# Gated linear attention and an ELU layer on one core: P3's bank and P5's sum, turns ahead of P7, squares and table load inside the layer, the weights' sums ahead of unit 2's layer

## The chip, the cores and the metric

The kernel runs on one core of one Trainium2 chip. The core has a matrix engine (TensorE, PE in the profile), a vector engine (VectorE, DVE), an engine for activation functions and copies (ScalarE, ACT), a general engine (GpSimd, POOL) and an engine that issues most of the transfers (SyncE, SP). Each works through its own list of instructions in order, and they wait for each other by semaphores. The metric is the device time of one execution, in microseconds (us). Lower is better.

## The reference

The first half is a gated linear attention with a complex decay. For 4 sequences of 8 heads, 768 steps and 48 channels per head:

```python
mag = sqrt(a_re*a_re + a_im*a_im);  scale = minimum(mag, 0.999) / (mag + 1e-6)
a_re_n, a_im_n = a_re*scale, a_im*scale
for t in range(S):                       # S_re, S_im: 48 x 48 per head
    new_re = ar*S_re - ai*S_im;  new_im = ar*S_im + ai*S_re
    S_re, S_im = new_re + outer(k[t], v[t]), new_im
    y[t] = q[t] @ S_re
```

The heads are then laid side by side, which gives x of 3072 tokens by 384, and the second half is

```python
h = x @ w_in                             # 384 x 2048
g = where(h > 0, h, exp(minimum(h, 0)) - 1)
out = g @ w_out                          # 2048 x 384
```

All is in float32.

## The kernel before, in words

**Units.** The work is cut into 12 units of two sequences and 128 steps each, numbered 0 to 11. A unit goes through three stages: the attention, which gives x; the layer, which multiplies x by w_in and applies the ELU, and gives g; and the products, which multiply g by w_out. Units 0 and 1 do layer and products directly (`inner`, `elu`, `project`). Unit 2 has the direct layer but the saving products, and units 3 to 11 have saving forms of both: fewer block products with sums of blocks before and behind.

**The attention of a unit.** `squares` (L709, L710, ACT) squares a_re and a_im, `joined` (L716) adds them, `logarithms` and `powers` take logarithms and exponentials (each with a load of the activation table), `ratios`, `lengths` and `slopes` work on them (DVE), `angles` (L815, ACT) takes the arctangent, `carried` (L826, DVE, one row) adds what the unit before left. `turned` (called by `turns`) sums the angles along time by a matrix product (L837, PE) and takes off whole turns (L842, L845, DVE), and `carry_on` (L862, POOL) stores the last row for later. `waves` (L973, L976, L977, ACT) makes sine and cosine. `decays` gives the decay factors E and F, `ends` (L957, POOL) loads the decays at the chunks' ends, `scaled` (L982 on POOL for k, L992 on DVE for q) multiplies by them, and `gated` (L1003, DVE for q, POOL for k) multiplies by the waves. Then q and k are transposed on PE (L1023) and copied by ACT (L1024), `scored` and `valued` make scores, states and outputs, and `seam` moves rows into place by transfers. `noted` (L796, L799, DVE) keeps the extremes of a for a later test, and the tiles of a exist once, so that `load_a` of the next unit waits for the last reader of this one, which is `noted`.

**The layer of units 3 to 11.** `mixed` and `mixed_rest` (L1409, L1429, DVE; L1432, POOL) make sums of x's blocks. Twenty multiplications (`mult`, L1449, four matrix products each, in the order of `ORDER`: 8, 1, 6, 3, 9, 7, 5, ...) add into five PSUM banks called b, z, w, x and y. Three of the banks come from a ring of three ("mlp") that the products also use. Where a bank's sum is wanted before more is added to it, ACT copies it (`kept`, L1462): z after multiplications 8 and 1, ahead of 3, and w after 6. `joint` (L1465, DVE) combines, and `low` and `whole_of` (L1470, L1471, L1474) apply the ELU, which needs the table of exponentials (`table`, L1200). The weights' side needs block sums too: 19 sums of w_in (`summed_in`) and 8 of w_out (`combined`, L1278), made once on DVE. `opened` takes over buffers that were in use before, for some of these.

**The products of units 2 to 11.** Seven block products, P1, P4, P2, P5, P6, P7, P3 in this order, each in two halves (`product`, L1319). P1 and P2 add up in columns 0 of the first bank and P6 takes columns 1 of it; P5 has columns 0 of another bank and P7 columns 1; P4 has the third. P3 adds onto P5. ACT copies P1 (L1327), DVE adds P6 to it (u2), then P7 (u3, L1344), and the four quarters of the output are: P1 + P2 (L1338, ACT), u2 + P5 + P3, u3 + P5 and u3 - P4 (L1340, DVE). Each goes out by a transfer (L1341).

**Order.** The order of the work is written by hand. A list, `first`, gives the beginning up to unit 2's layer. Behind it every step has a time in slots (`put`), 16 slots for a unit, and the steps are issued in the order of these times, each onto its engine. Unit u starts from r = 16(u - 2). While unit w's layer runs (r + 36 to r + 44) and its products (r + 44 to r + 52), the attention of unit w + 2 is under way at the same slots: with its own r, the products of unit w lie at r + 12 to r + 20, and the layer of unit w + 1 at r + 20. The turns of unit w + 2 at r + 18.32 so come behind P7, and the squares of unit w + 3, at its own r + 3.4, come just before the layer of unit w + 1. Between these, parts of the weights are fetched again and tested for small values (`test_fetch`, L666 and L669, SP; `test`, L680, DVE): 48 of them.

Of the kernel before, what the change touches and what calls it, by code (L numbers as in the profile page):

```python
# [13 lines left out]
ALU = mybir.AluOpType  # L14
# [491 lines left out]
def kernel(  # L506
# [12 lines left out]
    nc = tc.nc  # L519
# [53 lines left out]
    def work(shape, tag="w"):  # L573
        return ps.tile(shape, FP32, tag=tag, bufs=3, name=tag)
# [4 lines left out]
    def where(u):  # L579
        return u % (B // NB) * NB, u // (B // NB) * C  # L580
# [78 lines left out]
    done, tested = [], []  # L659
# [33 lines left out]
    def new(tag, bufs=1, shape=None):  # L693
        return sb.tile(shape or [C, NB, H, D], FP32, tag=tag, bufs=bufs, name=tag)
# [314 lines left out]
    PAIRED = 2  # L1009
# [239 lines left out]
    HN = DM // 2  # L1249
    spare, P = [], NF // 2  # L1250

    def Y(j, n):
        return w_out.rearrange("p (m j) n -> p m j n", j=2)[:, :, j, ts(n, HN)]
# [12 lines left out]
    def T_of(k, h):  # L1266

        if k == 4:
            return spare[4 + h]
        return (spare[2] if k == 1 else spare[3] if k == 2 else Y(0, 1))[:, ts(h, P // 2)]  # L1270
# [9 lines left out]
    def X(u, h, i, j):  # L1280
        return nat[u]["g", h].rearrange("p (m j) (i t) -> p m j i t", j=2, i=2)[:, :, j, i]

    def S_of(u, k, h):

        if k == 3:
            return spare[1][:, 0 : P * C].rearrange("p (m t) -> p m t", t=C)[:, ts(h, P // 2)]
        return X(u, h, *{1: (1, 0), 2: (0, 0), 4: (0, 1)}[k])
# [11 lines left out]
    def product(u, k, h):  # L1299

        x = nat[u]
        bank, n, first = {
            1: (0, 0, True), 2: (0, 0, False), 6: (0, 1, False), 5: (1, 0, True),
            7: (1, 1, False), 3: (1, 0, False), 4: (2, 0, True),
        }[k]
        if first and h == 0:
            x["p", bank] = work([C, 2, HN], "mlp")
        to = x["p", bank][:, n]
        a = {
            1: lambda: X(u, h, 0, 0), 2: lambda: X(u, h, 0, 1), 3: lambda: S_of(u, 4, h),  # L1310
            4: lambda: X(u, h, 1, 1), 5: lambda: S_of(u, 1, h), 6: lambda: S_of(u, 2, h),
            7: lambda: S_of(u, 3, h),
        }[k]()
        if k < 4:
            b = Y(*((0, 0), (1, 0), (1, 1))[k - 1])[:, ts(h, P // 2)]
        else:
            b = T_of({4: 4, 5: 1, 6: 2, 7: 3}[k], h)
        for m in range(P // 2):
            nc.tensor.matmul(  # L1319
                to, lhsT=a[:, m], rhs=b[:, m], start=(first and h == 0 and m == 0), stop=False,  # L1320
                skip_group_check=True,
            )
        if h == 0 or k in (4, 5):
            return
        if k == 1:
            x["u"] = new("ee", 2, [C, 2, GT])
            nc.scalar.copy(out=x["u"][:, 0, 0:HN], in_=to)  # L1327
            return
        u2, u3 = (x["u"][:, n, 0:HN] for n in range(2))
        if k == 6:  # L1330
            nc.vector.tensor_tensor(out=u2, in0=to, in1=u2, op=ALU.add)
            return
        seq, at = where(u)

        def done(i, n, a, b, op=None):
            o = new("o", 2, [C, HN])
            if op is None:
                nc.scalar.copy(out=o, in_=a)  # L1338
            else:
                nc.vector.tensor_tensor(out=o, in0=a, in1=b, op=op)  # L1340
            nc.sync.dma_start(out=out[ds((seq + i) * S + at, C), ts(n, HN)], in_=o)  # L1341

        if k == 7:
            nc.vector.tensor_tensor(out=u3, in0=to, in1=u2, op=ALU.add)  # L1344
            done(1, 1, u3, x["p", 1][:, 0], ALU.add)
            done(1, 0, u3, x["p", 2][:, 0], ALU.subtract)
        elif k == 2:
            done(0, 0, to, None)
        else:
            done(0, 1, to, u2, ALU.add)  # L1350


    ROLES = (1, 0), (1, 1), (0, 0), (0, 1)
# [125 lines left out]
    def verdict():  # L1479
# [31 lines left out]
        out=ident, in_=ident, pattern=[[-1, C]], base=0, channel_multiplier=1,  # L1511
# [42 lines left out]
    def put(at, fn, *args):  # L1554
        if fn is hidden:
            plan.append((at, len(plan), inner, args))
            plan.append((at, len(plan), elu, args))
        else:
            plan.append((at, len(plan), fn, args))

    def decays_of(u, *at):
        fns = squares, joined, logarithms, powers, lengths, ratios, slopes, noted, angles, carried
        if u > 3:
            put(at[6] + 0.3, carry_back, u)
        put(at[0], begun, u)
        for x, fn in zip(at, fns):
            put(x, fn, u)

    def gates_of(u, *at):
        for x, fn in zip(at, (decays, turns, waves, scaled, ends, gated)):  # L1570
            if fn is not decays or u <= PAIRED:
                put(x, fn, u)
# [47 lines left out]
        (ratios, 3), (project, 0, 0, 8, 12), (transposed, 2, "k", 0), (transposed, 2, "q", 1),  # L1620
        (slopes, 3), (angles, 3), (project, 1, 1, 12, 16), (transposed, 2, "k", 1),
        (carried, 3), (scored, 2), (turns, 3), (project, 0, 1, 8, 12), (valued, 2), (seam, 2),
        (noted, 3), (project, 0, 0, 12, 16), (waves, 3), (scaled, 3), (ends, 3),
        (project, 0, 1, 12, 16), (opened,),
    ]
    def layer_of(u, at_h, at_p):
        if u == PAIRED:
# [33 lines left out]
        for m, (k, h) in enumerate(ks):  # L1661
            put(at_p + m * step, product, u, k, h)
# [3 lines left out]

    for u in range(2, NU):
        r = (u - 2) * SLOTS
        put(r + (1.5 if u > PAIRED else 8), load_a, u)
        put(r + 8, load_v, u)  # L1670
        put(r + 8, load_qk, u)
        if u == 2:
            decays_of(u, 16, 16, 17, 17, 18.4, 19.5, 19.6, 22.7, 19.8, 19.8)
            gates_of(u, 20.4, 21.6, 22.1, 22.4, 22.4, 22.6)
        else:
            sq = (r + 7.2, r + 9.6) if u == PAIRED + 2 else (r + 3.4, r + 5)
            decays_of(u, *sq, r + 12.8, r + 13.2, r + 13.4, r + 13.5, r + 14.9, r + 15.7, r + 15.52, r + 16.6)
            gates_of(u, r + 15, r + 18.32, r + 18.5, r + 18.6, r + 18)
            put(r + 19.7, gated, u, None, ("q",))
            put(r + 19.8, gated, u, None, ("k",))  # L1680
            if u > PAIRED + 1:
                put(r + 19.45, table, "exp_and_others", u)
                put(r + 15.5, table, "trig_and_small", u)
            if u > PAIRED + 1:
                put(r + 16.8, scaled, u, "k", None)
        if u > PAIRED:
            for n in range(NB):
                put(r + 22 + 2 * n, transposed, u, "q", n)
                put(r + 23 + 2.3 * n, transposed, u, "k", n)
            at = r + (31.3 if u + 1 < NU else 30.6)  # L1690
            put(r + 28.2, scored, u)
            put(at, valued, u)
            put(at, seam, u)
            put(r + 34.45, mixed, u)
            put(r + 35.75, mixed_rest, u)
        layer_of(u, r + 36, r + 44)
    for n in range(len(SUMS)):
        put(37 + 0.6 * n if n < 11 else 45.4 + 0.6 * (n - 11), summed_in, n)
    for m, x in enumerate(((1, 0), (2, 0), (1, 1), (4, 0), (2, 1), (4, 1), (3, 0), (3, 1))):
        put(37.2 + m * 0.6 if m < 6 else 40 + m, combined, *x)  # L1700
    for m in range(NR):
        put(40 + 2.75 * m, test_fetch, m)
        put(42.2 + 2.75 * m, test)
    put(NU * SLOTS, verdict)
    items = [(fn, tuple(args)) for fn, *args in first]
    items += [x[2:] for x in sorted(plan, key=lambda x: x[:2]) if x[2:] not in items]
# [38 lines left out]
```

## Time and profile before

| | |
|---|---|
| runs of the kernel | 701.9 us median of 3 (700.37 to 706.64) |
| profiled execution | 701.03 us, of which the span is 699.3 us |
| mean granted clock of TensorE | 0.973 |
| PE, matrix products | 651.5 us busy, 93% of the span |
| DVE | 498.9 us, 71% |
| ACT | 418.9 us, 60% |
| POOL | 156.5 us, 22% |
| transfers | 56.12 MB, mean 80 GB/s |
| chain that ended last | PE 58%, DVE 15%, ACT 14% of the span |
| first multiplication of the layers of units 3 to 11 | 228.00, 278.69, 331.77, 388.60, 443.17, 495.98, 550.33, 604.39, 654.04 us |

A page of the profile shows one execution. The span is the time from its first instruction to its last. Each engine's busy time is the union of its instructions. The rows of slices cut the span into 40 equal pieces, and a digit is the busy share in tenths, or for PEclk the share of full clock that TensorE was granted. In the waits, "A <- B: total, times, longest" says that A's engine was idle until B ended. In the timeline a row has the start, the length, the engine, the line and operation, and in brackets the idle time of the engine ahead of it and what ended it.

### The profile page before, as it was taken

What the parts mean: (1) busy time and instruction counts of PE and PEld (TensorE: products, weight loads), DVE (VectorE), ACT (ScalarE), POOL (GpSimd) and SP (SyncE); (2) the same over time, 40 slices, a digit from 0 to 9 for tenths busy, and PEclk for the clock granted to TensorE, in tenths of its full rate; (3) what the DMA queues carried; (4) which work ended last, traced back from release to release, by engine and by line L of the source; (5) the groups of instructions that cost most, each with busy time, mean ns of one, the idle gap of its engine ahead of it and who ended that gap; (6) DMA issues with size and microseconds to landing.
All of it is one profiled execution on the core that took longest, in us unless ns stands there. A gap on an engine that the chain in (4) does not pass through costs nothing.

```text
span 699.3 us, 17222 instructions
## 1 busy us (share of the span) xinstructions
PE 651.5 (93%) x7236; PEld 591.3 (85%) x7236; DVE 498.9 (71%) x790; ACT 418.9 (60%) x684; POOL 156.5 (22%) x200
## 2 busy tenths in 40 slices
PE   8898889999997999899799899899899899999995
PEld 6777776577886998898799899899899899899995
DVE  5889999863979587487477668578568658755381
ACT  6875446847753775765567577477377477472250
POOL 2000000122114324324304403503502501502000
PEclk9899999999998999999899999999999999999999
DMA  9985646322815605603433242342620641210000
GB/s 167 169 162 104 157 137 177 57 64 45 136 39 79 119 17 98 122 17 70 97 70 74 72 75 64 74 100 60 125 51 24 129 71 31 60 31 13 18 1 29
DMA packets 151443, 56.12 MB, mean 80 GB/s; under 512 B 129684, under 2 KB 143164, under 8 KB 151356
## 3 DMA queue, kind: packets, MB, share of 16 engines
q1 hardware_dynamic: 147616, 53.58, 38.1%
q0 software_dynamic: 3520, 1.20, 1.5%
q8 instruction: 59, 0.97, 0.6%
q14 instruction: 28, 0.23, 0.1%
q10 hardware_dynamic: 220, 0.14, 0.1%
HBM read 48.91 MB, written 4.80 MB: 77 GB/s over the span
## 4 chain that ended last, share of the span: by engine, by line
PE 58%; DVE 15%; ACT 14%; issue 4%; DMA 4%; SPq 4%; ACTq 0%; DVEq 0%
PE mlp L1319 13%; PE mlp L1449 11%; PE y L1449 8%; PE mlp L1210 6%; PE w L1023 5%; PE mlp L1235 3%; SPq L598 3%; PE y L1235 3%; PE w L1064 3%; PE y L1109 2%; DMA ai<-in_a_im_dram 2%; PE y L1136 2%; ACT L1200 2%; DVE g L1297 1%; ACT L735 1%
## 5 line engine op out<-in xcount | busy, mean ns | idle before, releaser
L1319 PE MATMUL mlp<-w_out,g 128*128 128x192 f32 x640 | 116.2, 333 | 2.8 <-DVE o L1340 2.8
L1319 PEld LDWEIGHTS mlp<-w_out,g 128*128 128x128 f32 x640 | 106.8, 194 | 6.5 <-DVE o L1340 5.1
L1081 POOL TENSOR_TENSOR S<-S,T 128x384 f32<-128x384 f32 x36 | 33.1, 920 | 198.0 <-DVE S L1079 198.0
L1465 DVE TENSOR_TENSOR g<-g,mlp 128x512 f32<-128x512 f32 x45 | 30.9, 686 | 59.5 <-PE mlp L1449 42.1
L1210 PE MATMUL mlp<-x,w_in 128*128 128x256 f32 x288 | 65.1, 381 | 3.2 <-DVE g L1221 2.3
L1210 PEld LDWEIGHTS mlp<-x,w_in 128*128 128x128 f32 x288 | 53.8, 190 | 11.9 <-DVE g L1221 2.7
L1297 DVE TENSOR_TENSOR g<-g 128x512 f32<-128x512 f32 x80 | 59.4, 753 | 5.7 <-PE mlp L1319 4.7
L1449 PE MATMUL mlp<-x,w_in 128*128 128x128 f32 x432 | 58.9, 281 | 0.0
L1319 PE MATMUL mlp<-w,g 128*128 128x192 f32 x320 | 54.7, 329 | 0.0
L1449 PEld LDWEIGHTS mlp<-x,w_in 128*128 128x128 f32 x432 | 54.5, 198 | 0.0
L1319 PEld LDWEIGHTS mlp<-w,g 128*128 128x128 f32 x320 | 51.8, 190 | 0.7
L1474 DVE SCALAR_TENSOR_TENSOR g<-ee,g 128x512 f32<-128x512 f32 x63 | 43.8, 696 | 11.2 <-ACT ee L1471 11.1
L1024 ACT COPY qt<-w 128x512 f32<-128x512 f32 x48 | 25.9, 589 | 40.7 <-PE w L1023 40.7
L1470 ACT ACTIVATE ee<-g 128x512 f32<-128x512 f32 x63 | 39.5, 627 | 17.3 <-DVE g L1465 16.9
L973 ACT ACTIVATE cs<-n 128x768 f32<-128x768 f32 (+1 forms) x14 | 10.5, 751 | 63.6 <-DVE n L845 63.6
L1471 ACT ACTIVATE ee<-ee 128x512 f32<-128x512 f32 x72 | 45.4, 631 | 2.3
L1190 POOL DMA_DIRECT2D x<-y x62 | 29.9, 489 | 59.5 <-ACT y L1126 37.2
L1449 PE MATMUL mlp<-halves,g 128*128 128x128 f32 x144 | 22.5, 305 | 17.9 <-ACT g L1462 17.9
L1449 PEld LDWEIGHTS mlp<-halves,g 128*128 128x128 f32 x144 | 19.8, 213 | 19.4 <-ACT g L1462 19.4
L904 ACT ACTIVATE n<-w 64x384 f32<-64x384 f32 (+1 forms) x60 | 28.1, 486 | 8.9 <-PE w L889 8.3
L1462 ACT COPY g<-mlp 128x512 f32<-128x512 f32 x36 | 20.4, 586 | 21.3 <-PE mlp L1449 21.2
L1449 PE MATMUL y<-x,w_in 128*128 128x128 f32 x216 | 31.9, 295 | 0.0
(218 smaller groups left out, 1442.3 us busy)
## 6 DMA issues: line engine op xcount, KB each, us to landing
w<-in_moe_w_out_dram SPq DMA_DIRECT2D x8, 768.0 KB, 4.4
g<-in_moe_w_in_dram SPq DMA_DIRECT2D x24, 256.0 KB, 3.1
g<-in_moe_w_out_dram SPq DMA_DIRECT2D x24, 256.0 KB, 2.9
w<-in_moe_w_in_dram SPq DMA_DIRECT2D x16, 288.0 KB, 5.7
vn<-in_v_dram SPq DMA_DIRECT2D x24, 192.0 KB, 4.3
out_dram<-o SPq DMA_DIRECT2D x48, 96.0 KB, 2.7
ar<-in_a_re_dram SPq DMA_DIRECT2D x22, 192.0 KB, 3.5
ai<-in_a_im_dram SPq DMA_DIRECT2D x22, 192.0 KB, 4.8
```

What stands on the lines that cost most here:

```text
L1023: nc.tensor.transpose(t[:, h], of, ident)
L1081: eng.tensor_tensor(out=new_s, in0=new_s, in1=wide, op=ALU.mult)
L1190: eng.dma_start(out=x["x"][ds(j * HP + D, G), i], in_=x["y"][ds(j * HP + i * G, G)])
L1210: nc.tensor.matmul(t[:, e], lhsT=w_in[:, i, ts(f + e, C)], rhs=x["x"][:, i], start=(i == 0), stop=(i == NI - 1),)
L1235: nc.tensor.matmul(x["o", n], lhsT=x["g", f // 8][:, f % 8, ts(n, C)], rhs=w_out[:, f], start=(f == 0), stop=(f == NF - 1),)
L1297: nc.vector.tensor_tensor(out=S_of(u, k, h), in0=a, in1=b, op=op)
L1319: nc.tensor.matmul(to, lhsT=a[:, m], rhs=b[:, m], start=(first and h == 0 and m == 0), stop=False, skip_group_check=True,)
L1449: nc.tensor.matmul(x["c" + c][:, ts(m, C)], lhsT=a[:, m], rhs=x["mix"][p], start=(p == BANKS[c][0] and m == 0), stop=False, skip_group_che ...
L1465: nc.vector.tensor_tensor(out=part(u, to), in0=part(u, a), in1=part(u, b), op=op)
L1470: nc.scalar.activation(out=e, in_=part(u, of), func=AF.Relu, scale=-1.0)
L1471: nc.scalar.activation(out=e, in_=e, func=AF.Exp, scale=-1.0)
L1474: nc.vector.scalar_tensor_tensor(out=part(u, to), in0=nat[u]["e", to], scalar=-1.0, in1=part(u, of), op0=ALU.add, op1=ALU.max,)
```

## The change

- `product`: P3 starts a sum of its own in columns 0 of the bank that P1 and P2 had. Behind P6, DVE makes one more sum, u4 = u2 + P5. The outputs are then P3 + u4, P7 + u4, and (P7 + u2) - P4, the last in two steps.
- `turns` and `waves` go from r + 18.32 and r + 18.5 to r + 17.2 and r + 17.4, ahead of P7; the gates of q and k go from r + 19.7 and r + 19.8 to r + 18.7 and r + 18.8, and `mixed_rest` goes one slot ahead, in front of P3's second half.
- `squares` and `joined` go from r + 3.4 and r + 5 to r + 5.08 and r + 6 for units from 6 on, and to r + 7.2 and r + 9.6 for unit 5. (Unit 4 had the latter already, and unit 3's are in `first`.) The table load behind them goes from r + 19.45 to r + 21.1 for units from 6 on.
- `load_a` of unit 5 goes from r + 1.5 to r + 4.5, and `noted` of unit 4 from r + 15.7 to r + 20.3.
- `opened`, three of the sums of w_in and six of the sums of w_out move into `first`, ahead of the end of unit 0's last product, so ahead of unit 2's layer.
- The weight tests start 14 slots later, and follow each other at 2.5 slots in place of 2.75.

```diff
-            7: (1, 1, False), 3: (1, 0, False), 4: (2, 0, True),
+            7: (1, 1, False), 3: (0, 0, True), 4: (2, 0, True),
         }[k]
-        if first and h == 0:
+        if first and h == 0 and k != 3:
             x["p", bank] = work([C, 2, HN], "mlp")
...
-        u2, u3 = (x["u"][:, n, 0:HN] for n in range(2))
+        u2, u4 = (x["u"][:, n, 0:HN] for n in range(2))
         if k == 6:
             nc.vector.tensor_tensor(out=u2, in0=to, in1=u2, op=ALU.add)
+            nc.vector.tensor_tensor(out=u4, in0=x["p", 1][:, 0], in1=u2, op=ALU.add)
             return
 
-        def done(i, n, a, b, op=None):
+        def done(i, n, a, *sums):
             o = new("o", 2, [C, HN])
-            if op is None:
+            if not sums:
                 nc.scalar.copy(out=o, in_=a)
-            else:
+            for b, op in sums:
                 nc.vector.tensor_tensor(out=o, in0=a, in1=b, op=op)
+                a = o
...
         if k == 7:
-            nc.vector.tensor_tensor(out=u3, in0=to, in1=u2, op=ALU.add)
-            done(1, 1, u3, x["p", 1][:, 0], ALU.add)
-            done(1, 0, u3, x["p", 2][:, 0], ALU.subtract)
+            done(1, 1, to, (u4, ALU.add))
+            done(1, 0, to, (u2, ALU.add), (x["p", 2][:, 0], ALU.subtract))
...
-            done(0, 1, to, u2, ALU.add)
+            done(0, 1, to, (u4, ALU.add))
...
-        (noted, 3), (project, 0, 0, 12, 16), (waves, 3), (scaled, 3), (ends, 3),
-        (project, 0, 1, 12, 16), (opened,),
+        (noted, 3), (project, 0, 0, 12, 16), (opened,), (waves, 3), (summed_in, 0),
+        (summed_in, 1), (combined, 1, 0), (combined, 2, 0), (summed_in, 2), (combined, 1, 1),
+        (combined, 4, 0), (combined, 2, 1), (scaled, 3), (combined, 4, 1), (ends, 3),
+        (project, 0, 1, 12, 16),
...
-        put(r + (1.5 if u > PAIRED else 8), load_a, u)
+        put(r + (8 if u == PAIRED else 4.5 if u == PAIRED + 3 else 1.5), load_a, u)
...
-            sq = (r + 7.2, r + 9.6) if u == PAIRED + 2 else (r + 3.4, r + 5)
-            decays_of(u, *sq, r + 12.8, r + 13.2, r + 13.4, r + 13.5, r + 14.9, r + 15.7, r + 15.52, r + 16.6)
-            gates_of(u, r + 15, r + 18.32, r + 18.5, r + 18.6, r + 18)
-            put(r + 19.7, gated, u, None, ("q",))
-            put(r + 19.8, gated, u, None, ("k",))
+            sq = (r + 7.2, r + 9.6) if u < PAIRED + 4 else (r + 5.08, r + 6)
+            noting = r + (15.7 if u != PAIRED + 2 else 20.3)
+            decays_of(u, *sq, r + 12.8, r + 13.2, r + 13.4, r + 13.5, r + 14.9, noting, r + 15.52, r + 16.6)
+            gates_of(u, r + 15, r + 17.2, r + 17.4, r + 18.6, r + 18)
+            put(r + 18.7, gated, u, None, ("q",))
+            put(r + 18.8, gated, u, None, ("k",))
             if u > PAIRED + 1:
-                put(r + 19.45, table, "exp_and_others", u)
+                put(r + (19.45 if u < PAIRED + 4 else 21.1), table, "exp_and_others", u)
...
-            put(r + 35.75, mixed_rest, u)
+            put(r + 34.75, mixed_rest, u)
...
-        put(40 + 2.75 * m, test_fetch, m)
-        put(42.2 + 2.75 * m, test)
+        put(54 + 2.5 * m, test_fetch, m)
+        put(56 + 2.5 * m, test)
```

More of the change, by code (lines that the diff above doesn't have):

```diff
@@ L1328, in product @@
             return
-        u2, u3 = (x["u"][:, n, 0:HN] for n in range(2))
+        u2, u4 = (x["u"][:, n, 0:HN] for n in range(2))
         if k == 6:
             nc.vector.tensor_tensor(out=u2, in0=to, in1=u2, op=ALU.add)
+            nc.vector.tensor_tensor(out=u4, in0=x["p", 1][:, 0], in1=u2, op=ALU.add)
             return
         seq, at = where(u)
-        def done(i, n, a, b, op=None):
+        def done(i, n, a, *sums):
             o = new("o", 2, [C, HN])
-            if op is None:
+            if not sums:
                 nc.scalar.copy(out=o, in_=a)
-            else:
+            for b, op in sums:
                 nc.vector.tensor_tensor(out=o, in0=a, in1=b, op=op)
+                a = o
             nc.sync.dma_start(out=out[ds((seq + i) * S + at, C), ts(n, HN)], in_=o)
         if k == 7:
-            nc.vector.tensor_tensor(out=u3, in0=to, in1=u2, op=ALU.add)
-            done(1, 1, u3, x["p", 1][:, 0], ALU.add)
-            done(1, 0, u3, x["p", 2][:, 0], ALU.subtract)
+            done(1, 1, to, (u4, ALU.add))
+            done(1, 0, to, (u2, ALU.add), (x["p", 2][:, 0], ALU.subtract))
         elif k == 2:
-            done(0, 0, to, None)
+            done(0, 0, to)
         else:
-            done(0, 1, to, u2, ALU.add)
+            done(0, 1, to, (u4, ALU.add))
     ROLES = (1, 0), (1, 1), (0, 0), (0, 1)
```

## The prediction

> **What bounds the kernel now.** I read the page's busy shares first, then the waits of TensorE alone, then the timeline of ACT and of PE around one of those waits, and last the granted clock there.
>
> ```profile
> PE 651.5 (93%) x7236; PEld 591.3 (85%) x7236; DVE 498.9 (71%) x790; ACT 418.9 (60%) x684; POOL 156.5 (22%) x200
> ...
> PEclk9899999999998999999899999999999999999999
> ```
>
> TensorE is the bound: 93% busy, and every other engine has room. So only two things can shorten the run: less idle PE, and fewer stretches at a lowered clock (the 8s of the clock row).
>
> ```profile
> PE mlp L1449 <- ACT g L1462: 17.9, 7, 3.8
> PE w L837 <- DVE n L826: 3.5, 1, 3.5
> PE mlp L1319 <- DVE o L1340: 2.8, 3, 1.1
> ```
>
> These are the three longest waits of PE: total us, times, longest. The first is one place in each of seven layers. The timeline shows it at the layer of 388.60 us, ACT first (start, length, what, idle before), then PE:
>
> ```profile
> 388.07 0.84 ACT L973 ACTIVATE cs<-n 128x768 f32<-128x768 f32 x1 [6.83 <-DVE n L845]
> 388.82 0.83 ACT L976 ACTIVATE cs<-n 128x768 f32<-128x768 f32 x1
> 389.69 0.94 ACT L977 ACTIVATE cs<-cs,quarter 128x768 f32<-128x768 f32 x1
> 390.53 0.83 ACT L709 ACTIVATE n<-ar 128x768 f32<-128x768 f32 x1
> 391.26 0.83 ACT L710 ACTIVATE n<-ai 128x768 f32<-128x768 f32 x1
> 392.11 1.28 ACT L1200 ACT_TABLE_LOAD   x1
> 393.40 1.07 ACT L1462 COPY g<-mlp 128x512 f32<-128x512 f32 x2
> ```
>
> ```profile
> 382.11 2.76 PE L1319 MATMUL mlp<-w_out,g 128*128 128x192 f32 x16
> 384.71 1.45 PE L837 MATMUL w<-n,sum_turns 128*128 128x384 f32 x4
> 386.00 2.76 PE L1319 MATMUL mlp<-w_out,g 128*128 128x192 f32 x16
> 388.60 1.05 PE L1449 MATMUL mlp<-x,g 128*128 128x128 f32 x8
> 389.50 1.06 PE L1449 MATMUL mlp<-halves,g 128*128 128x128 f32 x8
> 390.39 1.06 PE L1449 MATMUL mlp<-x,w_in 128*128 128x128 f32 x8
> 394.04 1.16 PE L1449 MATMUL mlp<-halves,g 128*128 128x128 f32 x8 [2.59 <-ACT g L1462]
> ```
>
> PE runs P7, the turns' product, P3, then the layer's first three multiplications, and stops: the fourth adds onto a bank that ACT must first copy (kept). ACT sat idle for 6.83 us until DVE had made the angles, then did sine, absolute value and cosine, two squares and a table load before the copy. The copy was wanted at 390.4 and began at 393.4.
>
> ```profile
> 391.40:394.00 2.60, 0.04 (x1) 0.00 (x0) 1.91 (x3) 2.57 (x4) 0.88 (x2) 1.00 0.11 38
> 394.00:399.30 5.30, 5.26 (x32) 5.26 (x33) 1.70 (x3) 0.69 (x2) 4.75 (x2) 0.68 0.15 49
> ```
>
> In this table by stretch the first figures are length and PE busy; the third from the right is the granted clock. After 2.6 us without work it is 0.68 for the next 5.3 us.
>
> **The change, part by part.**
>
> Turns ahead of P7. P6 ends at 382.11. The angles' row (DVE L826) ran 381.27 to 382.22, so L837 can start at about 382.37 (in the trace L837 at 220.08 followed L826's end at 219.94 by 0.15): a wait of 0.26 that is not there now. It ends at 383.66. The four DVE steps behind it take 2.2 us (385.84 to 388.04 in the trace); from 383.2, when the first half is there, they end near 385.4, where today they end at 388.04. P7's three results no longer stand ahead of them. ACT's three waves take 2.46 us (388.07 to 390.53) and are done by 387.9. P7 and P3 end at 388.86, the multiplications 8 and 1 at 390.65: ACT is free 2.8 us before the copy is wanted, 1.5 us in layer 4, where the table load stays ahead of it. So the wait goes in all seven layers, squares moved or not; moving them adds 2.9 us more cover. The carry DMA of turns now stands on POOL ahead of the two DMAs of ends (1.9 us of issue); what those bring is read only by the state sums of the next unit, over 30 us later.
>
> What the wait costs: the seven gaps are 2.60, 3.79, four of 2.59 and 1.12, together 17.9. To that comes the clock: it is at 0.50 for 6.8 us from 337.5 and for 3.4 us each from 395.5, 501.4 and 556.0, and at half speed half of that is lost, 3.4 + 3 x 1.7 = 8.5. Here a rule speaks against so large a sum: the Trainium skill, "TensorE: Matmul & The Clock Gate", Part 1, throttles only after an idle window of about 3.4 us. By it only the gap of 3.79 would cost clock, and the sum would be 21.3. But three of the five gaps of 2.6 us have a slow stretch behind them, so the row decides: 26.4. As a cross-check, layers 4 to 10 begin at 278.69, 331.77, 388.60, 443.17, 495.98, 550.33 and 604.39; with 53.08 - 2.75 = 50.33 as the undisturbed spacing (its layer lost only the gap), these six spacings hold 23.7 too much, and the 1.3 of layer 10 makes 25.0. I take 25.0.
>
> P3 in P2's bank, P5 added to u2. P3 need not wait for P7's results. Today L837 hides that wait (no gap at 386.00); with L837 gone from there it would be 0.84 a layer, as at 650.50 and 689.31, so this part pays for the first. But u4 reads P5 from the bank that P7 writes. The Trainium skill ("PSUM — Partial Sum Buffer", PSUM bank collisions) has banks guarded as a whole, other columns too, so P7 must wait for u4: two DVE additions behind P6, like the 0.84 above. By the skill that is 0.84, without its rule 0. In the products of units 2 to 9 L837 with its 1.29 us lies between and hides it; in those of units 10 and 11, which have no turns beside them, 0.84 is paid at P7 in place of P3: net 0. One more DVE addition per unit (0.3 us) lies beside PE. P2's copy by ACT is done some 12 us before P3.
>
> Squares and table within the layer. In layers 4 to 9 two squares (1.66) and, from layer 5, the table (1.28) stand between the two first copies and the copies of the q transposes. From the layer's start: second copy ends at 3.4, squares at 5.0, table at 6.3; the first half of the transposes is there at about 6.0. ACT falls 0.3 behind, and the copy before multiplication 12 has 0.1 of room (348.63 to 349.21, wanted at 349.33). The squares also need ai landed: in the trace it lands, where a landing is recorded, between 4.1 us before a layer's start and 3.1 after. Behind the squares on ACT stand the table, all transposes' copies and every later kept copy, and PE waits for those. On DVE the gate of q (1.75) and the pair sum (0.42) now stand ahead of P3's result, whose bank multiplication 7 takes: P3's result at about 4.2 after the layer's start, multiplication 7 wants it at 4.5. POOL's gate of k ends near 7.9, its transposes come at 8.0. Cost of these thin covers: 0 to 1.2 a layer (each being missed by a few tenths); I take 0.3, since layer 3 today, begun at 228.00 with nothing late, shows no gap above 0.2. 7 x 0.3 = 2.1. For unit 5 alone the squares stand between k's copies and the copy before multiplication 12, where ACT is already full: 1.7.
>
> Weights' sums ahead of unit 2's layer. Nine sums, three of 0.6 and six of 0.87, 7.0 us of DVE. They go where DVE idles today: 8.27 us before 166.81 (waiting for ACT L904) and 2.60 before 171.23. Cost 0. Out of the layer they free DVE: the gap of 0.80 at 195.80 (PE for DVE L1079) goes. The layer itself (166.66 to 190.99) has no gap now, so nothing is won in it. What matters comes at 216.56: PE waits 3.52 for L826, then 1.09 for P3's results, then runs slowly (0.50 from 221.5 for 6.8 us). From P6's end at 213.80 to the next layer at 228.00 are 14.20 us for 6.49 of work: 7.7 lost. The change takes two reductions (0.86 each) and a weight test (0.33) from before L826, but asks for it 2.6 us sooner. L826 ends between 215.7 and 217.1 with P6 at 213.0: the wait is 2.8 to 4.2 with 0 to 3.4 of clock behind it. I take 3.5 + 1.7 = 5.2, a gain of 2.5 (0 to 4.9).
>
> Load of a for unit 5 and weight tests later: the load has 9 us until its squares, with 6.4 from issue to landing at worst; tests leave 184 to 228 and squeeze a little later, where DVE has 29% free. 0.
>
> Sum: 25.0 + 2.5 + 0.8 - 7 x 0.26 - 2.1 - 1.7 = 22.7. The profiled execution took 701.0 (span 699.3 and 1.7 around it), 0.9 below the median: 701.0 - 22.7 = 678.3, and with that 0.9, 679 us.
>
> **The rivals.**
>
> Thin covers miss everywhere: 1.2 us in each of eight layers, 9.6 in place of 2.1, gives 687. For it: four covers of 0.1 to 0.4. Against it: they overlap, and a gap on one gives room to the next.
>
> The wait moves instead of going: L826 comes late each time, so PE waits at L837 as it now waits at the copy, about 2.6 in seven units (18 on top of 679), with 0 to 4 of clock: some 697 to 701. For it: unit 2's product, where just this happens today. Against it: in the other seven L826 ends 0.11 after P6, released by ACT L815, with DVE waiting for it.
>
> Slower: squares meet an unlanded ai inside the layer. Then ACT is blocked behind them, and copies that PE needs stop too. It breaks even with today once a load lands some 6.5 us after the layer's start, giving about 3 us of gap and 1 of clock in six layers; at 9 us it is 6 x 6.5 = 39 on top of 678, some 717. For it: one load in the trace (issued at 328.5 us, behind a weight test) lands 3.1 after its layer's start. Against it: the tests' new places put no test between most loads and what they wait for.
>
> The edit falling short (P3 still waiting, 0.84 x 7) would give 685, within the second case.
>
> **How the numbers follow.** Forecast 0.62 (671 to 684: unit 2's gain from 0 to 4.9, covers from 0 to 0.7, clock by chance), thin covers 0.20 (684 to 692), the wait moved 0.10 (692 to 703), slower 0.08. Range 671 to 692. About 1% (7 us) is what a measurement tells from no change. Faster by more 0.85, within it 0.07, slower 0.08.
>
> **What would show it.** PE's wait for the kept copy under 3 us in all; layers about 50.5 to 51 us apart; L973 at least 3 us before its layer's first multiplication; L837 after P6 with gaps of 0.2 to 0.4, and one of 3 to 4 near 213; no slow clock at layers' starts. It is wrong if PE waits at L837 by over 1 us in most units, if PE waits at multiplications 7 or 12 or at transposes by over 1 us a layer, or if ACT L710 waits for ai.

## The result, and the profile after

The changed kernel takes 680.6 us (median of four runs, 677.98 to 685.29), where the kernel before takes 702.25 (median of four, 700.37 to 706.64). The ratio is 0.969, with a 95% interval from 0.962 to 0.976: faster by about 22 us. The profiled execution took 677.98, its span 676.2. Two rows of its page, the busy shares and the granted clock:

```profile
PE 642.4 (95%) x7236; PEld 581.7 (86%) x7236; DVE 502.3 (74%) x800; ACT 419.1 (62%) x684; POOL 157.8 (23%) x200
...
PEclk9799999999998999999999999999999999999998
```

PE stays the bound and is busy for 9 us less, though it has the same 7236 instructions: what is gone is time at half speed (the mean granted clock went from 0.973 to 0.986). Between the start and the last slice only one slow slice is left. In the clock's records behind 100 us, before had six slow stretches ahead of the end; now there is one, of 6.8 us, from 214.0.

The first multiplications of layers 3 to 11 now stand at 224.43, 276.93, 327.33, 378.31, 428.58, 478.91, 530.41, 580.36 and 630.08. From the first to the last of them it is 405.7 us where it was 426.0: 20.4 of the 23.1 us of span. 3.6 were won ahead of layer 3, some of it chance (a slow stretch from 105.4 us, in code that did not change, is missing now), and 0.9 were lost behind layer 11.

The waits of PE after (total us, times, longest):

```profile
PE w L837 <- DVE n L826: 4.3, 1, 4.3
PE y L1450 <- ACT g L1463: 4.0, 4, 1.8
...
PE mlp L1319 <- DVE ee L1332: 1.8, 2, 0.9
```

The multiplications are at L1450 now and kept's copy at L1463, one line further down. The wait of 17.9 us ahead of the fourth multiplication is gone from the list. The one layer in detail, ACT and then PE (start, length, what, idle before):

```profile
376.51 0.94 ACT L977 ACTIVATE cs<-cs,quarter 128x768 f32<-128x768 f32 x1
380.29 0.59 ACT L1463 COPY g<-mlp 128x512 f32<-128x512 f32 x1 [2.85 <-PE mlp L1450]
381.18 0.59 ACT L1463 COPY g<-mlp 128x512 f32<-128x512 f32 x1 [0.31 <-PE mlp L1450]
381.67 0.85 ACT L709 ACTIVATE n<-ar 128x768 f32<-128x768 f32 x1
```

```profile
371.74 1.53 PE L837 MATMUL w<-n,sum_turns 128*128 128x384 f32 x4
373.11 5.36 PE L1319 MATMUL mlp<-w_out,g 128*128 128x192 f32 x32
378.31 1.05 PE L1450 MATMUL mlp<-x,g 128*128 128x128 f32 x8
...
380.98 1.10 PE L1450 MATMUL mlp<-halves,g 128*128 128x128 f32 x8
```

Now ACT waits for PE: it has finished the waves and is idle for 2.85 us until the sum that it copies exists. P7 and P3 run as one stretch of 5.2 us, and the fourth multiplication comes 2.67 us behind the first, with no gap.

### The profile page after: what moved, and what is told of

The parts are those of the page before. It is cut to its first block, busy times and chain, and to the rows that moved or that the text cites. A ratio compares the mean times of both kernels' runs of the same rounds, so it can differ in the third digit from the quotient of the medians.

```text
span 676.2 us, 17220 instructions
## 1 busy us (share of the span) xinstructions
PE 642.4 (95%) x7236; PEld 581.7 (86%) x7236; DVE 502.3 (74%) x800; ACT 419.1 (62%) x684; POOL 157.8 (23%) x200
## 4 chain that ended last, share of the span: by engine, by line
PE 53%; DVE 11%; ACT 9%; issue 4%; DMA 2%; SPq 0%; DVEq 0%; ACTq 0%
PE mlp L1319 18%; PE mlp L1450 9%; PE y L1450 6%; PE w L1023 4%; PE mlp L1210 3%; PE w L1064 3%; PE y L1109 3%; DVE g L1466 2%; PE w L837 2%; PE y L1136 2%; DVE g L1475 2%; PE mlp L1235 2%; ACT L735 2%; ACT n L746 1%; DVE g L1297 1%
## 5 line engine op out<-in xcount | busy, mean ns | idle before, releaser
L1319 PE MATMUL mlp<-w_out,g 128*128 128x192 f32 x640 | 113.3, 331 | 1.8 <-DVE ee L1332 1.8
L1210 PEld LDWEIGHTS mlp<-x,w_in 128*128 128x128 f32 x288 | 53.8, 190 | 11.3 <-DVE g L1221 2.8
L1297 DVE TENSOR_TENSOR g<-g 128x512 f32<-128x512 f32 x80 | 57.7, 731 | 5.0 <-PE mlp L1319 3.8
L1466 DVE TENSOR_TENSOR g<-g,mlp 128x512 f32<-128x512 f32 x45 | 30.7, 683 | 38.2 <-PE mlp L1450 23.9
L1450 PE MATMUL mlp<-x,w_in 128*128 128x128 f32 x432 | 57.2, 275 | 0.0
L1450 PEld LDWEIGHTS mlp<-x,w_in 128*128 128x128 f32 x432 | 52.6, 192 | 0.0
L1463 ACT COPY g<-mlp 128x512 f32<-128x512 f32 x36 | 21.2, 588 | 43.4 <-PE mlp L1450 43.2
L1450 PE MATMUL y<-x,w_in 128*128 128x128 f32 x216 | 29.3, 278 | 4.0 <-ACT g L1463 4.0
L1450 PEld LDWEIGHTS y<-x,w_in 128*128 128x128 f32 x216 | 26.2, 192 | 4.9 <-ACT g L1463 4.8
L1219 ACT ACTIVATE ee<-mlp 128x512 f32<-128x512 f32 x24 | 14.3, 595 | 25.6 <-PE mlp L1210 16.8
```

Of the source, the lines that this page charges most:

```text
L1210: nc.tensor.matmul(t[:, e], lhsT=w_in[:, i, ts(f + e, C)], rhs=x["x"][:, i], start=(i == 0), stop=(i == NI - 1),)
L1297: nc.vector.tensor_tensor(out=S_of(u, k, h), in0=a, in1=b, op=op)
L1319: nc.tensor.matmul(to, lhsT=a[:, m], rhs=b[:, m], start=(first and h == 0 and m == 0), stop=False, skip_group_check=True,)
L1450: nc.tensor.matmul(x["c" + c][:, ts(m, C)], lhsT=a[:, m], rhs=x["mix"][p], start=(p == BANKS[c][0] and m == 0), stop=False, skip_group_che ...
L1466: nc.vector.tensor_tensor(out=part(u, to), in0=part(u, a), in1=part(u, b), op=op)
```

## The experiments

The theory: what was lost before was ACT's lateness at the kept copy, and the clock behind it. The rivals: that the gain comes from the product's new banks, or from the weights' sums. The change has parts that can be undone, or done alone. The runs come from three rounds of measuring, in which the kernel before had medians of 702.25 (with the changed kernel), 699.72 (the first four below) and 700.92 (the last four). So a difference of 2 us between medians of different rounds tells nothing.

**The product alone.** On the kernel before, only P3's bank and u4:

```diff
-            7: (1, 1, False), 3: (1, 0, False), 4: (2, 0, True),
+            7: (1, 1, False), 3: (0, 0, True), 4: (2, 0, True),
...
+            nc.vector.tensor_tensor(out=u4, in0=x["p", 1][:, 0], in1=u2, op=ALU.add)
...
```

> Only P3's bank and P5's sum, on the kernel before; turns, squares, tables, sums and tests stay. If P7 must wait for u4 because both are in one bank, PE waits about 0.84 us between P6 and P7 in the products of units 3 to 11, since L837 stands behind P7 here: slower than before by about 0.84 x 8 = 7 us, some 708 to 710. If other columns of a bank are free, nothing changes: 701 to 703.

Measured: 708.18 us (706.1 to 712.34), ratio 1.012 (1.005 to 1.020). The waits of its PE:

```profile
PE mlp L1450 <- ACT g L1463: 19.3, 8, 2.6
PE mlp L1319 <- DVE ee L1332: 15.1, 10, 7.3
```

Alone this part costs time. P7 waits for u4 in each of the ten products: 0.84 to 0.98 where nothing else is in the way, and 7.3 in unit 2's, where u4 stands behind L826 in DVE's full queue. So in this program P7 does wait for a reader of other columns of its bank; whether the hardware would need that wait, no run shows. The kept wait stays: 2.59 in seven layers, layer 3 now among them, and 1.13 in one.

**All but the product.** The changed kernel with the product of before:

```diff
-            7: (1, 1, False), 3: (0, 0, True), 4: (2, 0, True),
+            7: (1, 1, False), 3: (1, 0, False), 4: (2, 0, True),
...
```

> The changed kernel with the product as before: P3 adds onto P5, u3 is back. With L837 ahead of P7, P3 follows P7 directly and has to wait for P7's results, about 0.84 us in each of the products of units 2 to 9 where the changed kernel has no wait: about 0.84 x 8 = 7 us over the changed kernel, some 687. If this part pays nothing, 679 to 682.

Measured: 684.9 us (682.18 to 688.46), ratio 0.978 (0.970 to 0.985).

```profile
PE mlp L1319 <- DVE o L1340: 8.4, 10, 0.8
```

P3 now waits 0.84 ten times, in place of 0.91 twice at P7. That is the expected 7 us in the waits. The medians lie 4 us apart, between the two cases, and their ranges overlap. What the expectation left out are the waits of the layer's y bank for a copy by ACT (L1449 <- L1462; L1450 <- L1463 in the changed kernel): they are 1.2 us in all here, and 4.0 in the changed kernel.

**All but the turns.**

```diff
-            gates_of(u, r + 15, r + 17.2, r + 17.4, r + 18.6, r + 18)
+            gates_of(u, r + 15, r + 18.32, r + 18.5, r + 18.6, r + 18)
```

> The changed kernel with turns and waves back behind P7 (18.32 and 18.5). If moving squares and table is enough for the kept copy: ACT's waves end 1.9 us after the layer's start and the copy is wanted at 2.0, so no wait in layers 5 to 10, about 1.3 in layer 4 where the table load stays ahead; but P7 follows P6 directly and waits 0.84 for u4 in seven units, while the wait of 4.3 us in unit 2's product shrinks to about 1.7 and its slow clock (3.4) goes: together about the changed kernel's time, 679 to 684. If it is the turns that pay, PE waits again for the kept copy, about 2.6 us in each of seven layers with slow clock behind: 697 to 702.

Measured: 691.29 us (689.86 to 693.07), ratio 0.986 (0.979 to 0.993): between the two cases, and 10.7 us above the changed kernel.

```profile
PE mlp L1319 <- DVE ee L1332: 13.5, 10, 5.5
PE y L1450 <- ACT g L1463: 4.5, 4, 1.5
```

The kept wait does not come back (2.1 us in two places, 1.0 in layer 3 and 1.1 in layer 4), so the first case had the mechanism right. Two costs were missed. In unit 2's product P7 stops for 5.5 us at u4, and the clock is slow behind it: the wait for L826 was not shortened to 1.7 but moved, since u4 stands behind L826 in DVE's queue. And an undisturbed unit takes 51.6 us where the changed kernel takes 50.3: side by side, PE loses 0.8 at P7 and 0.5 within the layer and behind it, 0.4 of that at the transposes, whose gates come later when the turns do.

**All but the squares and the table.**

```diff
-            sq = (r + 7.2, r + 9.6) if u < PAIRED + 4 else (r + 5.08, r + 6)
+            sq = (r + 7.2, r + 9.6) if u < PAIRED + 4 else (r + 3.4, r + 5)
...
-                put(r + (19.45 if u < PAIRED + 4 else 21.1), table, "exp_and_others", u)
+                put(r + 19.45, table, "exp_and_others", u)
```

> The changed kernel with squares and table of units 6 to 11 back ahead of the layer. By the prediction the turns alone give enough room: waves end 0.9 us before the layer's start, squares 0.8 after, table 2.1 after, the copy is wanted at 2.0: a wait of 0.1 to 0.2 in layers 5 to 9, together within 2 us of the changed kernel, 679 to 682. If the squares' move is what pays: over 1 us in each of six layers, 688 or more.

Measured: 680.1 us (677.14 to 681.35), ratio 0.971 (0.965 to 0.978): the changed kernel's time. Squares begin 0.95 ahead of the layer, and the kept copy comes 1.98 behind its start, as in the changed kernel, though ACT now has no idle time left before it. With the turns moved, moving the squares brings no time that these runs can tell.

**Squares and table alone**, on the kernel before, for units from 6 on:

```diff
-            sq = (r + 7.2, r + 9.6) if u == PAIRED + 2 else (r + 3.4, r + 5)
+            sq = (r + 7.2, r + 9.6) if u == PAIRED + 2 else (r + 5.08, r + 6) if u > PAIRED + 3 else (r + 3.4, r + 5)
...
-                put(r + 19.45, table, "exp_and_others", u)
+                put(r + (19.45 if u < PAIRED + 4 else 21.1), table, "exp_and_others", u)
```

> The kernel before with one thing changed: squares of units 6 to 11 at 5.08 and 6, and their table load at 21.1. Turns stay behind P7, product as before. If the kept copy only needs the room on ACT, which either move gives: waves end 1.9 us after the layer's start, the copy is wanted at 2.0, no wait in layers 5 to 10, 1.1 in layers 3 and 4; L837 goes on hiding P3's wait; unit 2's product keeps its 7.7 us: before less some 20 to 23, so 677 to 682, as good as the whole change. If turns and product are needed for the gain: over 688.

Measured: 680.82 us (679.23 to 682.71), ratio 0.971 (0.966 to 0.976). Two lines give what the whole change gives, with loads, weight tests and sums all where they were, so that none of these is needed for the gain. ACT at one of its layers:

```profile
434.30 0.94 ACT L977 ACTIVATE cs<-cs,quarter 128x768 f32<-128x768 f32 x1
435.21 0.58 ACT L1462 COPY g<-mlp 128x512 f32<-128x512 f32 x1
436.10 0.58 ACT L1462 COPY g<-mlp 128x512 f32<-128x512 f32 x1 [0.31 <-PE mlp L1449]
```

The copy follows the cosine directly, just in time for PE, and undisturbed layers are 50.4 us apart. PE still waits 2.36 for it in layer 3, where 1.1 was expected, and 1.13 in layer 4, whose squares did not move, and 3.1 in six places for POOL's gate of k. L837 is still behind P7, where it hides P3's wait, and nothing has to wait for u4. The turns' move and the product's new banks then bring no time that can be measured on top. Each of them costs time without the other, as the first three runs show (in the second by 4 us, with ranges that overlap), and the whole change has waits of its own, 4.0 at the y bank. The last two runs take waits out of the changed kernel; whether this smaller edit could be brought as far was not tried.

**Without the weights' sums' move.** `opened` and the nine sums back where they were, the rest as changed:

```diff
-        (noted, 3), (project, 0, 0, 12, 16), (opened,), (waves, 3), (summed_in, 0),
...
+        (noted, 3), (project, 0, 0, 12, 16), (waves, 3), (scaled, 3), (ends, 3),
+        (project, 0, 1, 12, 16), (opened,),
```

> The changed kernel with opened and the nine weights' sums back in unit 2's layer. By the prediction: 7 us of DVE come back beside a layer without gaps, the gap of 0.8 at L1064 comes back, and the wait for L826 in unit 2's product (4.3) grows by 0 to 2, as DVE waits for ACT once in between: 1 to 3 us over the changed kernel, 681 to 684. If the sums' move carries the gain: over 690.

Measured: 682.67 us (679.29 to 684.05), ratio 0.974 (0.970 to 0.979), not to be told from the changed kernel. A gap of 0.59 comes back at L1064; the wait for L826 is 4.31, as in the changed kernel. Seven microseconds of DVE in that layer were free: in the wait for ACT's logarithms behind it DVE is idle for 3.55 us with the sums and without them.

**The wait for L826.** In the changed kernel's unit 2 product, DVE and then POOL:

```profile
212.24 2.62 DVE L826 SCALAR_TENSOR_TENSOR n<-n 1x768 f32<-1x768 f32 x1
```

```profile
212.22 1.81 POOL L982 TENSOR_TENSOR k<-k,n 128x768 f32<-128x768 f32 x1
```

L826 takes 0.95 in every other unit. Here it begins together with POOL's scaling of k and ends 0.83 behind it. The same meeting is in the kernel before, where it fell on a sum of w_in ahead of L826, which takes 0.68 elsewhere:

```profile
215.76 2.11 DVE L1397 TENSOR_TENSOR w_in<-w_in 128x512 f32<-128x512 f32 x1
```

```profile
215.49 1.82 POOL L982 TENSOR_TENSOR k<-k,n 128x768 f32<-128x768 f32 x1
```

The run takes the row out of this meeting, and puts it ahead of four other DVE steps:

```diff
-            decays_of(u, *sq, r + 12.8, r + 13.2, r + 13.4, r + 13.5, r + 14.9, noting, r + 15.52, r + 16.6)
+            decays_of(u, *sq, r + 12.8, r + 13.2, r + 13.4, r + 13.5, r + 14.9, noting, r + 15.52, r + (15.53 if u == PAIRED + 2 else 16.6))
...
-        put(37 + 0.6 * n if n < 11 else 45.4 + 0.6 * (n - 11), summed_in, n)
+        put(37 + 0.6 * n if n < 11 else 49.2 + (n - 14) * 0.05 if 14 < n < 18 else 45.4 + 0.6 * (n - 11), summed_in, n)
```

> The changed kernel with unit 4's row L826 ahead of four DVE steps (r + 15.53) and three weights' sums behind its turns. L826 then runs before POOL's scaling of k starts. If the 4.3 us are DVE's queue, and the 2.6 us of L826 come from that scaling beside it: L826 takes 0.95, PE waits about 1 at L837 and 0 to 1 at P7, and the slow clock there (3.4) goes: 4 to 6.5 us less than the changed kernel, 674 to 677. If L826 waits for what it reads (the carry's transfer or the angles): no change, 680.

Measured: 676.84 us (676.14 to 677.36), ratio 0.965 (0.960 to 0.970), 3.8 below the changed kernel's median, a little less than expected; all its runs lie below those of the changed kernel.

```profile
213.59 0.95 DVE L826 SCALAR_TENSOR_TENSOR n<-n 1x768 f32<-1x768 f32 x1 [0.69 <-DMA n<-carry]
```

L826 takes 0.95 again, PE waits 1.01 and 0.24, and there is no slow clock. Measured from P6's end, L826 ends 3.3 us sooner: 1.7 of this is its own length, the rest its place in DVE's order. From P6's end to layer 3 it is 8.7 us where it was 13.7. What is missing stands at layer 3: the sums moved behind the turns hold up DVE's results of the product, and PE waits 0.43 and 1.05 for L1341.

**The waits of 1 us ahead of multiplication 12.** In the changed kernel's layer 8, SP, DVE and PE:

```profile
476.89 6.46 SPq L1343 DMA_DIRECT2D out_dram<-o  x3
483.40 3.59 SPq L669 DMA_DIRECT2D g<-in_moe_w_out_dram  x2
```

```profile
486.15 0.42 DVE L680 TENSOR_REDUCE seen<-g 128x1 f32<-128x256 f32 x1 [3.16 <-DMA g<-in_moe_w_out_dram]
```

```profile
490.79 1.16 PE L1450 MATMUL y<-x,w_in 128*128 128x128 f32 x8 [0.99 <-ACT g L1463]
```

P3's result now stands behind the gate of q and the pair sum on DVE. Its transfer to the output blocks SP until 483.4, the fetch of a weight test stands behind that, DVE stops 3.16 us for the test, and what DVE should have made for ACT is late: PE waits 0.99. The run, on top of the last one:

```diff
-        put(56 + 2.5 * m, test)
+        put(56.45 + 2.5 * m, test)
...
-            sq = (r + 7.2, r + 9.6) if u < PAIRED + 4 else (r + 5.08, r + 6)
+            sq = (r + 7.2, r + 9.6) if u < PAIRED + 3 else (r + 9, r + 10) if u == PAIRED + 3 else (r + 5.08, r + 6)
```

> carry_early, and each weight test 0.45 slots later, and unit 5's squares at r + 9. If the waits of about 1 us ahead of multiplication 12 in layers 8 and 10 come from DVE waiting for a test's transfer that SP issued late, and the 1.8 in layer 3 from squares waiting for ai: all three go, 3 to 4 us less than carry_early, 670 to 674. If they come from the squares and tables among ACT's copies: no change in layers 8 and 10, at most 1.8 in layer 3.

Measured: 673.68 us (median of six runs, 672.03 to 674.11), ratio 0.961 (0.957 to 0.964). From layer 3 to layer 11 it is 404.2 us against 407.3 in the run before it. The waits in layers 3, 8 and 10 are gone; one of 0.50 has come in layer 6. In layer 8 DVE still stands idle for a test (2.23 us), but one sum for ACT (L1466) now goes ahead of it. The run has two edits; they are told apart only by place, since unit 5's squares lie in layer 3. This is the fastest version, and faster than both kernels: its six runs lie below all four of the changed kernel.

## Why the prediction was right

Forecast were 679 us within 671 to 692, measured 680.6. What bounded the kernel, and how the wait would go, were right. In the profiled pair, though, the total was met partly by luck: at unit 2's product 2.0 us of the forecast are missing, and the slow stretch at 105.4 that did not come back gave about 1.7. Step by step:

- The kept wait and its clock, 25.0: right. ACT was to be free 2.8 us before the copy is wanted; it was free 2.85 before. From layer 4 on, the spacing is 49.7 to 50.4 us in five of seven, near the 50.33 of the forecast, and the clock's slow stretches at the layers' starts are gone with the gaps. In this the row was the better guide than the rule that the prediction quoted: the 20.4 gained between layers 3 and 11, with what was lost there (1.8 at L837, 3.9 ahead of multiplication 12), make 26.1, near the row's 26.4 and not the rule's 21.3. The clock's part, an estimated 8 (26.1 less the 17.9 of gaps), was not measured by itself, and it is not fixed: of the seven gaps of 2.59 us in the run with the product alone, three had a slow stretch at their end.
- "Squares moved or not": right, by the run without their move. The prediction did not see the reverse, that the squares and table alone are enough, and so it gave the turns and the product a part in the gain that the runs do not show to be needed.
- 0.26 a unit at L837: right; P6's second half takes 2.86 us up to L837's start, where it took 2.60.
- The bank guard, 0.84: right in size (0.84 to 0.98) and place, hidden by L837 in units 2 to 9 and paid in the products of units 10 and 11 (0.91 each).
- Thin covers, 2.1: the size was met (0.15 + 0.99 + 1.11 = 2.25), the cause was not, so the size was luck. It was not the squares (without their move the waits are 0.70 and 1.35), nor multiplication 7's bank, but a weight test waiting for its fetch. The step that failed is "tests leave 184 to 228 and squeeze a little later", put at 0, together with the one that weighed P3's later result for its bank only: SP's queue behind that result was left out.
- Unit 5's squares, 1.7: measured 1.78. ACT waited 0.44 for ai there, at L710. That is one of the prediction's own signs of being wrong, but it came in this one unit only.
- Unit 2's product, a gain of 2.5 (0 to 4.9): measured 0.5 (14.20 us from P6's end to layer 3 became 13.74). The mis-sized term is the wait with its clock, 3.5 + 1.7. The wait was 4.31, just outside the given 2.8 to 4.2. The slow stretch of 6.8 us began 1.0 before the wait's end, so about 2.9 was lost behind it. L826 ended 6.1 us behind P6's end before and 4.2 now, against 2.7 to 4.1 worked out. It began 1.55 behind P6's end where it had begun 5.20, but POOL's scaling of k, which before held up a step ahead of it, now held up L826 itself.
- Sums at no cost, and 0.8 won at L1079: the gap went, but the time of the run without their move is the same within what the runs can tell.

## What to carry to other kernels

Two edits that each give the late engine room at the same wait do not add up: try each alone before keeping both, since the simpler one may be enough (here two lines gave 680.8 us, the whole change 680.6). When a result is moved back in one engine's queue, follow its transfer too, and what is queued behind that transfer. A bank of PSUM was one resource in this program: a sum read from one half of it held back the matrix product that writes the other half, by 0.84 to 0.98 us.

## What was not expected of the hardware

A DVE instruction on a single partition (L826, 0.95 us) took 2.62 us when it began together with a POOL tensor operation of 1.81 us, and 0.95 again when it ran ahead of one. It is not alone: in the traces of before and after, 23 DVE instructions took over 1.25 times their usual time. Each of them ran beside a POOL tensor operation, and each reads two inputs from SBUF, the large on-chip memory (L1297 took 1.20 in place of 0.68). DVE instructions with a single input or with one in PSUM kept their usual time beside POOL (L680 0.41, L845 0.56).

And gaps of 2.6 us on PE were followed by half clock in three of five cases before the change, and in three of seven with the product alone.
